# Cross-shaped window attention: the halves of a score tile lose their mutual waits on VectorE, and TensorE's steps are put in another order

## Chip, core and metric

The kernel runs on one core of one Trainium2 chip. The metric is the device time of one execution in microseconds (us); of several runs the median is given. TensorE (PE in the profile) does the matmuls, ScalarE (ACT) the exponentials, VectorE (DVE) and GpSimd (POOL) the elementwise work, and SyncE (SP) starts most of the DMAs.

## The reference

The input is one image `x` of 224 x 224 tokens with 96 channels. One matmul gives q, k and v. The first 48 channels are attended to within 28 horizontal stripes of 8 rows, the last 48 within 28 vertical stripes of 8 columns. A stripe has 1792 tokens, and each of its tokens attends to all 1792. Cut to what matters:

```
qkv = einsum('bhwc,cd->bhwd', x, wqkv);  q, k, v = thirds of qkv
scale = 48 ** -0.5
# horizontal: stripes of 8 x 224 tokens, channels 0..47
ah = softmax(einsum('bqc,bkc->bqk', qh, kh) * scale);  oh = einsum('bqk,bkc->bqc', ah, vh)
# vertical: stripes of 224 x 8 tokens, channels 48..95
av = softmax(einsum('bqc,bkc->bqk', qv, kv) * scale);  ov = einsum('bqk,bkc->bqc', av, vv)
out = einsum('bhwc,cd->bhwd', concat(oh, ov), wo)
```

The exponentials are the bulk of it: 56 stripes of 1792 x 1792 scores.

## The kernel before

**Passes and tiles.** Two stripes make a pass, and there are 28 passes: 14 horizontal, then 14 vertical. Within a pass the query columns are cut into four chunks (512, 512, 512, 256). A score tile is 128 keys of both stripes against one chunk, 128 partitions x 1024 columns: columns 0 to 511 belong to the one stripe, 512 to 1023 to the other. A pass has 49 tiles. Of these, 41 go to ScalarE, which takes `exp` of the whole tile in one instruction (L796). The other 8 go to VectorE and GpSimd, which work out an exponential by a polynomial: six of kind P and two of kind R, 224 tiles in all.

**The polynomial tiles.** VectorE takes each in halves of 512 columns, one half for each PSUM bank; `emit_p` records one such half. Pass p1 (L834) reads a bank and writes a half of a buffer `qb`. For kind R, pass p2 (L836) reads the same bank and that half of `qb` and writes a half of the tile `PT`. Then GpSimd works on all 1024 columns (`mids`: L846, L849 and L850 for kind P, L848 for kind R). Later TensorE computes the scores of the tile a second time, into two banks, and pass f (L839) joins them with `PT`. So VectorE has 448 instructions of p1, 112 of p2 and 448 of f.

**Waits.** Nothing is waited for by address. `Sched.commit` records each instruction with the keys that it reads and writes; `deps` turns them into waits on a counter of each engine. An instruction of VectorE that writes a key which VectorE wrote before waits for that earlier one too: only TensorE is let off waiting for itself. A `fresh` key forgets its past. Before the change, one buffer `qb` has one key, `("q", n)`, and one tile `PT` has one key, `("PT", slot)`, whichever half is touched.

**Order.** TensorE's steps stand in the strings of `ORDER`, one letter a step: `q` the scores of a ScalarE tile (L635), `1` and `2` the first and second scores of a polynomial tile (L648), `v` the product with V (L661), `k` a step that prepares the next pass (L437, L454, L483, L501), `f` a step of the output projection (L537, L573). The other engines' orders follow from it: as the letters are gone through, a planner with assumed durations (`D_H` for a half) and due times (`dve_step`, `pool_step`, `advance`) decides in which order VectorE and GpSimd take what has become ready. All engines then run their queues in order and wait on the counters.

**Buffers.** ScalarE's tiles use two sets of two PSUM banks. Four banks (`RING`) serve all the rest; `1` and `2` take two of them at once, and they come free as VectorE reads them out (L834, L836, L839, L813, L459, L470, L508, L443, L552, L585). There are 24 tiles `PT` and 5 buffers `qb`.

**DMAs.** SyncE's queue, in order, loads `x`, writes the transposed `x` to DRAM in the horizontal passes and reads it back in the vertical ones, and writes the output rows after L585; the last few output rows alternate between SyncE's and ScalarE's queue.

Of the kernel before, what the change touches and what calls it, by code (L numbers as in the profile page):

```python
# [30 lines left out]
D_MM, L_MM, L_PV, L_FILL = 0.216, 0.465, 0.44, 0.215  # L31
W_PE, W_FIN = 0.021, 0.08
SEMD, SEMP, SELF, SEMX = 0.15, 0.10, 0.19, 0.05
D_H, D_SQ, D_AF, D_ML = 0.6, 1.9, 1.03, 2.08


COLD = 8.0
# [3 lines left out]

KIND_OF = [0, 0, 0, 0, 0, 0, 0, 0, 0, 0, 0, 0, 0, 0, 0, 0, 0, 0, 0, 0, 0, 0, 0, 0, 0, 0, 0, 0]
ORDER = [
    "kqkqkkq11qkqkq1qvvvqkvqqkvq1vqkkqvkq1qkkqkq2qvkvq2vqv2qkvq1qvqvvvqvvq2qkvvqkvq1vvq2qvvq2kqvkv1qqvkkqvvkqvvkq2qvvkvq1qvkv",
    "fqv2qvvq1vqv1qvqvkqvvqvfqvvq1kqvq1fqvvvq1vqvvqvvq2qvkq2qkvq2qkvqv2qvvvqv1qvkqkvqvkq2kvq2qkvvqkq1vqkvkqffqvvvqkkqvvvfq1qvvvq2vk",
    "qvq2vvkqq1vvvvqkq1vqvqvkqkvq1qvv2qvfqvkvqvfqv1qvkqvvkq1qkvvvqkq2qvvq2qfkvqvqk1qvvfqkvqv2qfvqv2qvq1vqkvvfq2qvvkvq2qvvvvvkqq2vvfqk",
    "vvq1vvq1qvvkq1qvvvqvvqkvqkq1vqv1qvq2vvqv2qvqkq2vvvq1qvvvvqkqvvvqkkqfkqvvq2kq1qkvvqkqfvq2vvq1qvvkq2qvkvqkvkq2qvvvqffqvvkqvvvq1qv",
    "1qkqkvq2vqv1qvvfqvvqfqvvqkvq1fqvvq1vqv2q2qvvqv2qvv1qvqvvqvkq1qvv2qkqvvvfq2qvvvkqvqk2qvkvvq1qvvvkq2qkvvqkkvvqqkvkvv1qfqvvvkqv2qkvvq",
    "1qvffqvkqv1qvvqvvqvvq1vqkq1vqv2qkvqv2qkqvffqkvqvfqv2qvvq1vfqvqvvvqvvvq2qkvvq1qvvkkqfqv2qvkqfvq2vvq1qvkvqv2qkqkvqkvqvfq1vvqvkqvkkvv",
    "v2qvq1vvqffqkqvvvq1vqkvvqqkvkvq2q1qvvq2vvq2vqvkkvq1qvvkvq1qkvvvvqfkqvvqv2qvq1vvq2fqqkvvffqvvq1vq2qvkqvvq1qkkqkq2vvvq1qvvvkq2qkvvq1",  # L50
    "vqvkqvvqvvq1vvqffqvkqkkvq2qvvvq2vqvkkqkvvq1qkvvq2vvqvfq2vqvvfqvvq1qkvqvqvkvq1vq1qvkqv2qkvqv1qvkqvkq2qvkvq1qfvqvvvq2fqvvvqvkvq2qvv1",
    "qqvvvqv1qkqvvq1qvkq1vqvvqkqkfqvq2vqkvqkkvqv2qvvkqv2qvvq2vqkqvkq1vqkvqv2qvvvqv1qkqvkvq2fqvvqkvqvf1qvvqvkqv2qvvvq2qvvkfqvvfqv1",
    "qvqvkq2qvfqv1qvvqvvqvkqvfqv2qvkqvkq1qvvkvq1qvkvq2vqv1qvvqvvqkqfvkqvvq2vqkvq1vqv2qvkqfvqv1qvkqkvq2qvvfqvffqvvqkvqvkq2vqvkqvkf",
    "fqkvqvq1vvq1qvvkq2qvvkqvkq1qvvvqvvq1qvv2qvvq1qvkvq2qvvkq2qvkqfkvvq1qvvvqkqvvq1vvkqvq2vkqvq2vkqvvkq2qvvv1qkvqvvq2qkvvqv1qkvvvq1qv",
    "v2qfqvv1qvqvkqvqvk1qqkvvkq1qvv2qvvq1vvqvfqvkqvvqfkqvkvqkvq1kq2qvvv2qfqvkvqkqvvq2vqv2qkvqv1qvkqvkvq2qvvfqv2qvvvqk1qvvqkvvqfffqvvvqv",
    "1qvkqvkq2qkfqvvq2vqkvq1qvvqvvqv1qvvqkfq2qvvkqkqvkkqvvq1kq2qvkvfqvvq1qvvqvvvqkqk1qvvvq1qvvvq2kqvvq2vqvkq2vqvkqkvvq1fqvvvvq1qfvv",
    "q1qvvqvvq2vq2qvvq1qvvfqvvq2vqv2qvvq2fqvvkqvq1vfqvkqvkqv2qvvq1vkqvvvqkqv1qvvqvvkq2qkvvq2qfvvvq1qvvkqv1qvvfqkqvvvkq2qvvvkqvkfqvq2",
    "vvvq1qfvvvq1qvvqvvvq1qvqvkvq2qvfq2qvvkq2qvq1qkfqvv1qvqvvkqvvfqvq2vqkvvq2qvv1qvqkkfqfqvvvq2vqv1qkvqvqkvkqvkqvvq2vqvvkvq2fqvvvqv",
    "1qfvvqq1vvqfqvvqfvqv1qvvqvqvvq1vqkkvqkvq1q2qvq2q1qkvqvvvq2vqvvq1qvkfqvvqv2qkqvkvq2qkvvq1qvkvq2qvvkvq1qvvkvqvqvvvkq2fqvvvq",
    "v2qfqvvv1qvvq1qvfqvvvqqvvvqkqkk1qq2q1qvvvq2vvq1qvvqvvvq2qfvqq1vkqvvqf1qkqkkq2qvvvq2qvv1qfqvkqkvvvq2qvkvfqkqvvfqvqvv2vqfqkvvvv",  # L60
    "q1qvv2qfqvvvvq1qvvvvqfqqvvq1vvq2qkfqvvvq1qvvq1qvvvvqvq2vqvkq2qkvqkvq2vqv1qkvfqvq2vvqkkqv1qvq2vvq2qvvkqkkvvqq1vvkqvv1qvfqkvvvq2",
    "vqv1qvvqvqv1qvvqfvqvfqvvvq2qkkqvvqv2qvvvq1kqvq2vqv1qkvqvfqkqvq1vqvvvq1qkvqvv2qkqkqvv2qkvqkfqkvqvvq2qvv1qvvqvkqfvvqv2qvfqvv",
    "fqvqv2vqv1qvq1vvqvvqv2qvvqvqkkqkvfqkvqvfkqq1vvvvq1qvkvq2vqkvq2qvv1qvqvvqkvvq2qvq1vqfkqvvq2vvq2qvvq1vqkvvqkvfqvq2vvqvv1qkvqv2q",
    "vq1vq1qvvvqvqvvvq1fqvqfvqvvfqkvqqv2qvvq2qv2qvvkqfvq1vqvvqkvqkv2qkqvkq1vqvvqkqvvq1fqvq2vqkqv1qvvq2qvkqkvkqkvqv2qvvq1vvvq",
    "2qvv1qfvfqvvqfqvvvq1qvvvqvqvvvq1kqkq1qkqf2qvqvvqfkvvq2qvvvq2vq1qvvqvvqvq1kq1fqvqvvv2qvvq2kvqqkv2qkqkvvkq2qvvvvq2fqvvvkqfqvkvvqvvv",
    "q1fqvvq1vqvqv1qvvqvvvqvvq1qkkkqvvq2qvvkqv1vqv2qq1fqvqvvqkvq2vqv1qvq2qfvvqvqfvvq1vqvv2qfqvvvkqvkq2qkqkvvqvkkvq2qvvv2qfqvvvkvqfv",
    "qv1qvvvq1qfvqvfqvvqvvvkq1qvvqkvqvvqkv2qkvq1qvq2kq1qv2qq1qkvqvvvqkvq2qvvqkkvq1qfvvqv2qvvvq2qvkvvq1qvvvvqkvq2fqvvfqvvqkvvvq2qvv",
    "1qvvq1qfvvqvq1vqvvfqvq1qvqkvqvvkqkfqkvqv2qq1q1qvvqvvvq2qvq2kqv1qvvqkvvq1qvv2qvfqvkqvvq2vqvkq2qkvkqvkqkvqv2qvvq1vfqvvqfv",
    "vq2vqq1fqvvvq1vqvvqfqvvqvvvq2vqq1vqvkkqvkq2qkvq1qkfqvq2qfkqkvvqq2vvq1qkvqvvqvkvq2qvvvq1vvq1qvvkvq1qfvqvv2qvv1qvkqvqkvvv2qf",
    "vqvvq1qvvqvq2fqvqvv1qvq1qfvqvvvq2vqvv2qfqkvvqkvvqkqkvvq2kqvq1vkqvvqkqvvvq1vq1qvvqv2qvvq2vqkvqfvq2vqvkqvfqvvvvq2qvvkqvkq1vqvk",  # L70
    "1qfqvvvvq2vfqvvq1vqvvqqvvvq1vqv2q1qvvqv2qfvqvqfvfqvvq2qfqvvvq1fqvvqvqvvqv1qvvq2vvq1vvq2qvvv2qfvqfqfvfqvvfqvvfq2qvvvv2qfqvvvvvvfqvqffvvfvvvvfff",
]
MRG, LATE, BLATE = 0.01, 0.1, 0.05

# [98 lines left out]
def bass_standalone__window_attn_cswin__vision_kernel(  # L173
# [28 lines left out]
    with es:  # L202
        es.enter_context(nc.allow_low_precision(reason="sums for a mean key, which is taken off every key alike"))

        def sb(name, shape, dt):
            return es.enter_context(nc.sbuf_tensor(name, shape, dt))
# [19 lines left out]
        PT = [sb(f"PT{i}", [128, 1024], BF16) for i in range(NPT)]  # L226
        qb = [sb(f"qb{i}", [128, 1024], FP16) for i in range(NQB)]
# [13 lines left out]
        def bank(bi):  # L241
            return ps[:, bi * 512:(bi + 1) * 512]
# [3 lines left out]
        def low16(bi):  # L246
            return bank(bi).bitcast(I16).rearrange("p (n t) -> p n t", t=2)[:, :, 0]
# [14 lines left out]
        S = Sched()  # L262
# [516 lines left out]
        begun = set()  # L779

        def pt_keys(slot):
            return [("PT", slot)]
        pv_total = {c: len([1 for p in pv_chunks_of if p == c]) for c in range(NCH)}

        def emit_fill(f, bi):
# [8 lines left out]
        def emit_qk(tl, s, slot):  # L794
            S.commit("pe", 0.0, D_MM, L_MM, qk_fn(tl, s, 2 if 1 <= ia[0] <= NTWICE else 1), kt_keys(tl), set_keys(s), fresh=set_keys(s))
            S.commit("act", 0.0, D_ACT, None, lambda e, s=s, slot=slot: e.activation(  # L796
                PT[slot][:], ps[:, 512 * SETS[s]:512 * SETS[s] + 1024], ACTF.Exp, scale=LN2),
                set_keys(s), pt_keys(slot), fresh=pt_keys(slot))
# [29 lines left out]
        def emit_p(what, tl, h):  # L828
            bi, cols = tl["bp"][h], slice(512 * h, 512 * h + 512)
            q, y = qb[tl["qb"]][:, cols], PT[tl["slot"]][:, cols]  # L830
            bk, qk, ptk = [("bank", bi)], [("q", tl["qb"])], pt_keys(tl["slot"])
            if what == "p1":
                m, a = (HS * 2.0 ** -16, HS * RB) if tl["kind"] == "R" else (2.0 ** -16, 0.5 + PK)
                fn, reads, writes = lambda e: e.tensor_scalar(q, low16(bi), m, a, ALU.mult, ALU.add), bk, qk  # L834
            elif what == "p2":
                fn, reads, writes = lambda e: e.scalar_tensor_tensor(  # L836
                    y.bitcast(FP16), low16(bi), -RA * 2.0 ** 16, q, ALU.add, ALU.mult), bk + qk, ptk
            else:
                fn, reads, writes = lambda e: e.scalar_tensor_tensor(  # L839
                    y.bitcast(U16), bank(bi), 128.0, y.bitcast(FP16), ALU.mult, ALU.add), bk + ptk, ptk  # L840
# [45 lines left out]
        def dve_step():  # L886
# [304 lines left out]
```

## Time and profile before

| | |
|---|---|
| median of 3 runs | 1124.3 us (1120.11 to 1124.32) |
| the profiled execution | 1120.92 us; its span, first to last instruction, 1119.0 us |
| granted TensorE clock, mean | 0.995 |
| first and last ScalarE exponential | starts at 9.8 us, ends at 1111.0 us |
| L796, exponentials of 128x1024, ScalarE | 1148 instructions, 1076.5 us busy |
| L834 (p1), L839 (f), halves of 128x512, VectorE | 448 each, mean 686 and 687 ns |
| L836 (p2), VectorE | 112, mean 689 ns |
| HBM | 35 GB/s over the span |

An engine's busy time is the union of its instructions' spans. On VectorE and ScalarE an instruction may begin before the one ahead of it has ended, so an instruction's duration is more than the time that it takes from its engine; the time from one start to the next tells that. 1120.92 us is 1.9 us more than the span, and 3.4 us under the median.

### The profile page before, as it was taken

The page shows a single profiled execution, that of the slowest core. Times are in us where ns is not written, and L with a number is a line of the kernel's source. Part 1 is how long each engine was busy: PE and PEld are TensorE (multiplying, and loading weights), DVE is VectorE, ACT ScalarE, POOL GpSimd, SP SyncE. Part 2 cuts the span into 40 slices and gives each one's busy share as a digit, 9 for nine tenths or more (in the row PEclk, how much of TensorE's full clock was granted, in tenths as well). Part 3 has the DMA queues.
Part 4 walks back from the last instruction along what each step waited for, and adds up shares of the span by engine and source line. Part 5 has one row for each costly group of instructions (what it writes and reads, how often), then busy time and mean ns, then how long its engine had stood idle before and what let it go on. Part 6 is the DMA issues. An engine that isn't in the chain of part 4 may idle for free.

```text
span 1119.0 us, 36142 instructions
## 1 busy us (share of the span) xinstructions
PE 1071.9 (96%) x14928; PEld 428.7 (38%) x14928; DVE 1071.6 (96%) x2298; ACT 1081.1 (97%) x1159; POOL 955.8 (85%) x597
## 2 busy tenths in 40 slices
PE   9999999999999999999999989999999999999997
PEld 4344443443433443443333333333333343333332
DVE  8999999999999999999999999999999999999997
ACT  7999999999999999999999999999999999999996
POOL 7999789978888779979988998887989778897984
PEclk9999999999999999999999999999999998999999
DMA  5222123212302230321000112101111120121012
GB/s 93 38 50 52 20 33 51 43 17 45 52 11 42 52 51 2 52 42 36 2 26 15 35 20 53 38 19 45 46 40 23 41 52 11 46 47 41 17 25 38
DMA packets 183805, 40.97 MB, mean 37 GB/s; under 512 B 180408, under 2 KB 180952, under 8 KB 183640
## 3 DMA queue, kind: packets, MB, share of 16 engines
q1 hardware_dynamic: 182376, 38.14, 17.8%
q8 instruction: 117, 1.92, 0.7%
q10 hardware_dynamic: 1264, 0.52, 0.2%
q14 instruction: 48, 0.39, 0.1%
HBM read 19.36 MB, written 19.27 MB: 35 GB/s over the span
## 4 chain that ended last, share of the span: by engine, by line
DVE 46%; PE 40%; ACT 5%; issue 5%; POOL 3%; DMA 0%; DVEq 0%; ACTq 0%; POOLq 0%
PE ps L661 15%; DVE qb L834 14%; PE ps L635 13%; DVE PT L839 12%; PE ps L648 5%; ACT PT L796 5%; DVE out_all L585 5%; DVE PT L836 4%; PE ps L454 3%; DVE OT_sb L813 2%; DVE KT_sb L459 2%; DVE xT_sb L443 2%; PE ps L501 2%; PE ps L537 1%; DVE V_sb L508 1%
## 5 line engine op out<-in xcount | busy, mean ns | idle before, releaser
L796 ACT ACTIVATE PT<-ps 128x1024 bf16<-128x1024 f32 x1148 | 1076.5, 1041 | 25.7 <-PE ps L635 16.6
L635 PE MATMUL ps<-QT_sb,KT_sb 49*64 49x512 bf16 (+1 forms) x5420 | 477.9, 362 | 10.1 <-ACT PT L796 6.5
L661 PE MATMUL ps<-PT,V_sb 128*49 128x512 bf16 (+1 forms) x3136 | 455.2, 362 | 1.5 <-DVE PT L839 0.4
L846 POOL TENSOR_TENSOR PT<-qb 128x1024 f16<-128x1024 f16 x168 | 316.7, 1893 | 107.8 <-DVE qb L834 70.1
L850 POOL TENSOR_TENSOR PT<-PT,qb 128x1024 f16<-128x1024 f16 x168 | 355.5, 2124 | 9.1
L839 DVE SCALAR_TENSOR_TENSOR PT<-ps,PT 128x512 uint16<-128x512 f32 x448 | 305.7, 687 | 14.0 <-PE ps L648 4.9
L834 DVE TENSOR_SCALAR qb<-ps 128x512 f16<-128x512 int16 x448 | 305.6, 686 | 11.1 <-PE ps L648 4.9
L635 PEld LDWEIGHTS ps<-QT_sb,KT_sb 49*64 49x64 bf16 x5420 | 147.6, 104 | 256.8 <-ACT PT L796 199.9
L661 PEld LDWEIGHTS ps<-PT,V_sb 128*49 128x49 bf16 x3136 | 134.1, 103 | 197.3 <-issue 152.3
L648 PE MATMUL ps<-QT_sb,KT_sb 50*64 50x512 bf16 (+2 forms) x1792 | 181.6, 395 | 18.2 <-DVE qb L834 3.9
L849 POOL TENSOR_SCALAR PT<-PT 128x1024 f16<-128x1024 f16 x168 | 175.3, 1043 | 14.3
L848 POOL TENSOR_TENSOR PT<-PT 128x1024 f16<-128x1024 f16 x56 | 106.0, 1893 | 15.4 <-DVE PT L836 11.2
L585 DVE SCALAR_TENSOR_TENSOR out_all<-ps,rc,Ph_sb 128x96 bf16<-128x96 f32 x392 | 97.5, 306 | 0.6
L648 PEld LDWEIGHTS ps<-QT_sb,KT_sb 50*64 50x64 bf16 (+2 forms) x1792 | 51.0, 104 | 107.1 <-DVE PT L839 31.4
L836 DVE SCALAR_TENSOR_TENSOR PT<-ps,qb 128x512 f16<-128x512 int16 x112 | 77.1, 689 | 4.2
L813 DVE CAST OT_sb<-ps 113x512 bf16<-113x512 f32 x112 | 68.7, 613 | 0.2
L470 DVE CAST QT_sb<-ps 128x512 bf16<-128x512 f32 (+1 forms) x111 | 66.9, 611 | 2.1 <-PE ps L454 1.9
L459 DVE TENSOR_SCALAR_CACHE_REDUCE KT_sb<-ps 128x512 bf16<-128x512 f32 x108 | 64.0, 613 | 0.2
L552 DVE TENSOR_TENSOR Ph_sb<-ps,rc 128x480 bf16<-128x480 f32 (+1 forms) x84 | 52.0, 619 | 1.4
L508 DVE CAST V_sb<-ps 128x480 bf16<-128x480 f32 (+1 forms) x84 | 50.2, 615 | 1.7 <-PE ps L501 1.5
L454 PE MATMUL ps<-xT_sb,wq_sb 97*64 97x512 bf16 x224 | 41.2, 369 | 1.2 <-DVE wq_sb L487 0.6
L454 PE MATMUL ps<-xT_sb,w_sb 97*64 97x512 bf16 x224 | 40.1, 370 | 1.5 <-DVE out_all L585 0.5
(63 smaller groups left out, 395.0 us busy)
## 6 DMA issues: line engine op xcount, KB each, us to landing
xT_sb<-xt_dram SPq DMA_DIRECT2D x28, 336.0 KB, 3.9
out_dram<-out_all SPq DMA_DIRECT2D x385, 24.0 KB, 1.9
out_all<-in_x_dram SPq DMA_DIRECT2D x52, 168.0 KB, 2.7
xt_dram<-xT_sb SPq DMA_DIRECT2D x26, 336.0 KB, 6.0
xt_dram<-xT_sb SPq DMA_DIRECT2D x4, 168.0 KB, 4.5
Ph_sb<-in_x_dram SPq DMA_DIRECT2D x2, 168.0 KB, 3.8
Ph_sb<-in_x_dram ACTq DMA_DIRECT2D x2, 168.0 KB, 4.0
out_dram<-out_all ACTq DMA_DIRECT2D x7, 24.0 KB, 1.9
```

The lines of the kernel that those rows point to most:

```text
L454: ins = e.matmul(bk[64 * w:64 * w + 64, 0:qs], lhsT=lw, rhs=xT_sb[b][:, w, q0:q0 + qs], start=True, stop=True)
L585: return e.scalar_tensor_tensor(out_sb[b][:, w, kt, :], bk3[:, s, 0:C], rc[ri][:, s:s + 1], Ph_sb[:, kt, j, :], ALU.mult, ALU.add)
L635: ins = e.matmul(bank(SETS[s] + w)[64 * kh:64 * kh + 64, i * t["qs"]:(i + 1) * t["qs"]], lhsT=KT_sb[b][64 * w:64 * w + CA, kt * 128 + 64 * ...
L648: ins = e.matmul(bank(bp[w])[64 * kh:64 * kh + 64, 0:512], lhsT=KT_sb[b][64 * w:64 * w + nr, kt * 128 + 64 * kh:kt * 128 + 64 * kh + 64], ...
L661: ins = e.matmul(bank(pb)[64 * w:64 * w + CA, 0:t["qs"]], lhsT=V_sb[b][:, w, kt, :], rhs=PT[slot][:, ca:ca + t["qs"]], start=st and i == 0 ...
L796: S.commit("act", 0.0, D_ACT, None, lambda e, s=s, slot=slot: e.activation(PT[slot][:], ps[:, 512 * SETS[s]:512 * SETS[s] + 1024], ACTF.Ex ...
L834: fn, reads, writes = lambda e: e.tensor_scalar(q, low16(bi), m, a, ALU.mult, ALU.add), bk, qk
L836: fn, reads, writes = lambda e: e.scalar_tensor_tensor(y.bitcast(FP16), low16(bi), -RA * 2.0 ** 16, q, ALU.add, ALU.mult), bk + qk, ptk
L839: fn, reads, writes = lambda e: e.scalar_tensor_tensor(y.bitcast(U16), bank(bi), 128.0, y.bitcast(FP16), ALU.mult, ALU.add), bk + ptk, ptk
L846: sq = lambda e: e.tensor_tensor(y, q, q, ALU.mult)
L849: af = lambda e: e.tensor_scalar(y, y, PB, 128.0 * PA, ALU.add, ALU.mult)
L850: ml = lambda e: e.tensor_tensor(y, y, q, ALU.mult)
```

## The change

The key of a buffer `qb` and the key of a tile `PT` are split in two, one for each half. `emit_p` reads and writes the keys of its own half alone; GpSimd (`mids`), ScalarE and TensorE (`pt_keys`) name both. `fresh` now clears the key of each half with that half's first write. `D_H`, the planner's duration of a half, goes from 0.6 to 0.608. `ORDER` is replaced as a whole: it has the same 3531 steps (1148 `q`, 224 `1`, 224 `2`, 1372 `v`, 387 `k`, 176 `f`) in another order, and with it the orders of VectorE, GpSimd and SyncE move. The number of instructions stays the same on every engine, and one output row goes from ScalarE's DMA queue to SyncE's (7 and 385 become 6 and 386).

```
-D_H, D_SQ, D_AF, D_ML = 0.6, 1.9, 1.03, 2.08
+D_H, D_SQ, D_AF, D_ML = 0.608, 1.9, 1.03, 2.08
...
 ORDER = [
-    "kqkqkkq11qkqkq1qvvvqkvqqkvq1vqkkqvkq1qkkqkq2qvkvq2vqv2qkvq1qvqvvvqvvq2qkvvqkvq1vvq2qvvq2kqvkv1qqvkkqvvkqvvkq2qvvkvq1qvkv",
...
+    "kkqkkq1qkqkkq1qvqkvq1kvqqvvkvqkq1qkvq1qkqkv2qvqk2qkvqkqv2qvvkq1qvvvqkvqvq1vvq1qkvqv2qvvq2vqkv2qvqkkqvkkqvvvvq2qkvvvqv2qvv",
...
         def pt_keys(slot):
-            return [("PT", slot)]
+            return [("PT", slot, 0), ("PT", slot, 1)]
...
         def emit_p(what, tl, h):
...
-            bk, qk, ptk = [("bank", bi)], [("q", tl["qb"])], pt_keys(tl["slot"])
+            bk, qk, ptk = [("bank", bi)], [("q", tl["qb"], h)], [("PT", tl["slot"], h)]
...
-            S.commit("dve", 0.0, D_H, D_H + SEMD, fn, reads, writes, fresh=writes if h == 0 and what != "f" else [])
+            S.commit("dve", 0.0, D_H, D_H + SEMD, fn, reads, writes, fresh=writes if what != "f" else [])
...
         def mids(tl):
...
-            qk, yk = [("q", tl["qb"]), "pser"], pt_keys(tl["slot"])
+            qk, yk = [("q", tl["qb"], 0), ("q", tl["qb"], 1), "pser"], pt_keys(tl["slot"])
```

More of the change, by code (lines that the diff above doesn't have):

```diff
@@ L43 @@
 ORDER = [
-    "kqkqkkq11qkqkq1qvvvqkvqqkvq1vqkkqvkq1qkkqkq2qvkvq2vqv2qkvq1qvqvvvqvvq2qkvvqkvq1vvq2qvvq2kqvkv1qqvkkqvvkqvvkq2qvvkvq1qvkv",
-    "fqv2qvvq1vqv1qvqvkqvvqvfqvvq1kqvq1fqvvvq1vqvvqvvq2qvkq2qkvq2qkvqv2qvvvqv1qvkqkvqvkq2kvq2qkvvqkq1vqkvkqffqvvvqkkqvvvfq1qvvvq2vk",
-    "qvq2vvkqq1vvvvqkq1vqvqvkqkvq1qvv2qvfqvkvqvfqv1qvkqvvkq1qkvvvqkq2qvvq2qfkvqvqk1qvvfqkvqv2qfvqv2qvq1vqkvvfq2qvvkvq2qvvvvvkqq2vvfqk",
-    "vvq1vvq1qvvkq1qvvvqvvqkvqkq1vqv1qvq2vvqv2qvqkq2vvvq1qvvvvqkqvvvqkkqfkqvvq2kq1qkvvqkqfvq2vvq1qvvkq2qvkvqkvkq2qvvvqffqvvkqvvvq1qv",
@@ L48 @@
[L48 to L71, printed above, removed]
+    "kkqkkq1qkqkkq1qvqkvq1kvqqvvkvqkq1qkvq1qkqkv2qvqk2qkvqkqv2qvvkq1qvvvqvkqvq1vvq1qkvqv2qvvq2vqv2qkvqkkqvkkqvvvvq2qkvvvqv2qvv",
@@ new lines @@
+    "q1vvq1qkvqvkq1vqkqvvqvvfqvvq1qkq1q2kqvvvq1qvvvqvvq2vqvkqfvq2vqv1qvvqv2qkvvqvkq2kqvffqkvqkfqvvq2qvvq1kqvvvq2qvkvqkfqvvkvq1qk",
+    "vvfqkvq2qkqffqvq1qv1qvqvkqvvq2q1qvvvvq1qvkvvq2qvvkvq1qvkvqvvqvkqv2qvfqkvvvq2qvvvvq1qkvvq2qkvvvq2qvvvkq1qkvfqkvqkvqkvvq1qvkvvqvfq2",
+    "vqkvq1qkvq2qvvffqvqvv1qkqkfqvqvvqv2qvvvq1fqvvkqvq2vvq2qvvkqkvq1qvvkq1kqvqvkvqvfqkqkkqvq1vqv2qvkvqkfqvkvvq1qv2qvvq2vvq1qvvvvvfq",
+    "qkvv2qvvqf1qvvvq2vqv1qvqkqq1qkqvvvq2vqv1qvvq2qk2qvqkvvkqkvq1qkvvvvvfqfqvvvvqfvq1qkvq2vvq2qvkvvqffqvvvkq1qvkvvq2qvkqkvvvvq2qvkvvvkvqfq",
@@ new lines @@
+    "v1vqv2qkqvvvqf1qkfqvqvkq2qkvq1qvvvqvvqv2qvq1qv1qkvqkvkqvq1vkqvqv2qvvqv1qvkq2qkvvvq2qvvkqv1qkqvv2qkqkvvq1qfvvqkkqvvq1vvvq1q",
+    "vvvvq2qqkkvq1qfvvfqq2vvq1qvv1qvvqkvqvvvqv1qq2kvqvvkq2vvq2qvvvkq2qkvvfqvfqkvvqv1qkvq2qvkvfqvqv2qvkqkqkkvq2qvkvvfqfqvkvvvqf1qvvvq1qvvq",
+    "1vqvvvqvq2vvq1qvvvvqffqvvvq2vvq2qkqvv2qkqkvq1qvv1qvqkvqvvq1vqv2qvvvq1kqfqvvqkkvqvvkq2qvkvq2fqvvvqkkqkqvvq2vqkvvqkvvq2qvvvkkqvvq1vqvv",
+    "1qvqkvvq1qvvkqvqvkqkq1vfqvvq2fq2qvqvv1qvq1vqkvqvvvqv2qvvfqv1qvqkvqvvkq2qvkfqvv2qvvq1qkfqv2qvvkqkvq1qfvvqvvkq2qvvvfqkqkvkqkfqvv1v",
@@ new lines @@
+    "qq2vkqvkq1vqvvqvvqkqfvq1vqkvq1vqv1qvvqvvqkvq2qvvq2vvqkkqv2qvvq2qvv1qvvqv1qkvvq2qkvvqffqvvkqkqv2qvkvq2qvvkvqfqvvvkqvkkqvvfq2qvv",
+    "v1qvq1fqvkqvvq1fqvvvqvvqkqkq1vqvkq2fqvvvqkvq2vqv2qvvq1vfqkqvvkq2qkvvvq1qkvvqvfqvvvq1qvkvqv2qvvq2vvq1qkvqkkqvvqkq2vqvvkqkvvfq2qvvvv1",
+    "qvqkfqvvqfkq1qkfqqv1qvvqvvqv2qvq1qkq1vqv2qvvq1vqkvvqvqkvqv2qfvqvvkqvkq2fqvvvvq2qkvvvq1qvv1qvkqvkq2qkvqvvqkvkqffqvvvkq1qkvv",
+    "qkvkq2vqv2qvvq1vqvvq1vqkqvvvqv2qvvqk1qkqfvqv2qfvqkvvq2qkvvvq1qkvvq1vkqvqvkvq1qvvvqkvq2vvvq2qvvkfqvvq2vqv1qkqkvvqkqvkfqkvvq2vqvvfqv2",
@@ new lines @@
+    "qvvq1qv1qvq1qvvvqvvqv1qfvqvfqv1q1qvqvvkqvvqvq2qvv1qkqvv2qvq2qkvvqv1qvvqkvq2kvq2qvvkqkvqffqvvkvq2qvkvqkvvqk1qvvvqffqvkvvvqfq",
+    "2qv1qvq2vqvffqvvqv1qvvvqvvqv1qvq2vqv1qvq2qvvkq1qvvqvvkqfq1qvvfqq2vqkvqvv1qvvq2qvvkvq2qvvkq2kqvfqvkqvkq1vqkqkvkvq2qvvvkvqfqvv",
+    "2qvvq1qvv1qvvqvvqvvq1vqfvqvvvqkq2fqkvqvvvq2vqvkqkvq2kq1qkvq1qvvqvvqvvkq2qkvvqv1qkqvv2qvvq1vqv2qvvq1vqkfqvkvqvvqvv2qfqvvvfqvkvqv",
+    "2qvvq1fqvvqvvq1vqvvfqvvqkqvvvqv2qvq1vqkvq2vvq2qvv1qkqvv1qkvqkqq1vvqvq1vqfkqkvqv2qvvq2vqkvq2qfvqkvkqvvq1q2qvvvfqkqvvvkqvfq2vv",
@@ new lines @@
+    "qvvq1qvvvq2vqv1qvvqfvqvvqv1qvvqv2qvvkqfkqvkqvvq2vqvvkq1vqvq1vqfqvvqvvqv1qfqq2vqvv2qfqkqvkq2vvq2qvvqk1qkqvfqkvvqkkqvq1vk",
+    "vqfqvv1qvvvq2qvv1qvqvvvq1qvvvqv1q2qvvqkvkq1qvvqvvq2qvv2qvfqkvvqkvfqkvqvvq1qkvfqkqvvvq2qfvvq2qvvq1vvq2qkvkqkqkvvvvq1qvvv1qkvvq2qvv",
+    "vq2fvqvfqvvvvqvvv1qvfqqqq2qkq1qfvqvkvvq1qkvqv1qkvqvkqvq2vvq2qvv2qkvqkqvvq1vvq1qvkfqvvqv2qvkqkvq2fqvqvkvqv1qfqvvvq2vqkvvfqv",
+    "q1vqvvq2vq2qvv1qvqvvvq1qvvvqv1qq22qvqvv1qvvqvqkvq1vqfkqvvvq2vqvkqv1qvvkqvfqkvq2qkvvq2vfqvvvq1qvvkqkvvq2qvvvq2vkvqq1vvkqkvkvvqfqvvv1",
@@ new lines @@
+    "qvvqvvq2qvvvqv1qvq1vvq2q2qvvq1vqvqkvvqfkqfqvvqvkqkvvq2kq1fqvvqvvq1vqfvqv2qvqvvkq2qvfqvvqvkqk2qvvqvvqf2qvvvqvq1kqvkqkvfqkv",
+    "vqvv1qfqvvvvqfvq1vqvvvqq1qfq2qvqvkqkvq2qvkvq2qvv1qfqkvvq2qvvvq1vqvfqvvqvkqv1qvvq1qkkqfvq2qvvvqkq2qv1qkvqvvkqkfqvvvvq2qvvvvk",
+    "q2fqvq1qvvqvvq1vqvvqvvvqk2q1qvqvkvq1vqkq1qvvqvvvq2vqv2qfqvvkqvvq1qvfqvvvq2qvkqv2qvvq1vvq2qkvvqkqv2qkvqkvqkvqkfqkvvq2vq",
+    "v1qvq1vfqvvqfvvqfvq1qvvqvqvvvqv1q2qvvvq1qvv1qqvkvqvvqk2qvvq2vqkvqkvq1vvqv2qfqkvvq2qvvkqv2qvvq1fqvvvqkqkvqk1qvvvq2qvvkqvvkqkfqv",
@@ L72 @@
+    "v2qvvq1qfvqfvvqvqv1qvvqvvqv1q2q2qvvqv2qvq1vvkqkqkvq1qvvvvqfkqvvqv1qkq1fqvvvqvv2qvqkkvq2qfvqvv2qvvvq1qvkqvvvkq2qvvvkvq2qkvvfqvkvq",
+    "v2qvfqvvvvq1qvvvvq1fqvvvqq1qq1qq1qvvqvq2qvv2qvqkvkq1qvkqfkvqvvq2qfkqvvvq1qvkvvq2qvv2qkvkqfqkvvvqvvq2fqvvvvq2vqvvkq1qvvkfqvkq",
+    "v1qvvqv1qvvvqvvqv1qvfqq2vqvfq1qvvvqv1qfqqvvvq2qvvqv2qfvqqv1qvvvq2vfqvvq2qvvfqvvq2vvq1qvvq2vqvvffqvfqvvffqvfqvvvq2vqvffqvvqvvfqffvvvvfvff",
 ]
```

## The prediction

> **What bounds the kernel now.** I read the page's busy times first, then VectorE's instructions in order of time, then TensorE's waits at the score steps, then two passes side by side. The page:
>
> ```profile
> PE 1071.9 (96%) x14928; PEld 428.7 (38%) x14928; DVE 1071.6 (96%) x2298; ACT 1081.1 (97%) x1159; POOL 955.8 (85%) x597
> DVE 46%; PE 40%; ACT 5%; issue 5%; POOL 3%; DMA 0%; DVEq 0%; ACTq 0%; POOLq 0%
> L796 ACT ACTIVATE PT<-ps 128x1024 bf16<-128x1024 f32 x1148 | 1076.5, 1041 | 25.7 <-PE ps L635 16.6
> L839 DVE SCALAR_TENSOR_TENSOR PT<-ps,PT 128x512 uint16<-128x512 f32 x448 | 305.7, 687 | 14.0 <-PE ps L648 4.9
> ```
>
> Three engines look full, and the chain of waits runs through VectorE most. Busy time doesn't tell them apart, since it counts waits inside a pair of instructions as well. VectorE in order of time does (start, length, instruction, count):
>
> ```profile
> 705.21 0.68 DVE L470 CAST QT_sb<-ps 128x512 bf16<-128x512 f32 x1
> 705.81 0.65 DVE L508 CAST V_sb<-ps 128x480 bf16<-128x480 f32 x1
> 706.41 1.42 DVE L834 TENSOR_SCALAR qb<-ps 128x512 f16<-128x512 int16 x2
> 707.74 2.73 DVE L839 SCALAR_TENSOR_TENSOR PT<-ps,PT 128x512 uint16<-128x512 f32 x4
> 710.39 1.11 DVE L508 CAST V_sb<-ps 128x480 bf16<-128x480 f32 x2
> ```
>
> L470 lasts 0.68 us, yet its successor starts after 0.60: instructions overlap. The pair L834 takes 1.33 us to the next start, the four L839 take 2.65, so not 2 or 4 times 0.61. By the starts, a half followed by an instruction that does not wait for VectorE gives its place up after 0.608 us (medians 607 to 609 ns); a half directly followed by its own second half, which waits for it, after 0.715 to 0.717 (L834 to L834, 159 times; L839 to L839, 165) or 0.725 (L836 behind L834 or L836, 84). So the wait costs 0.11 us each time.
>
> VectorE's load is the sum of its start-to-start times without waits: 1008 halves x 0.608 = 613; 248 copies of 512 columns x 0.60 = 149; 83 of 256 x 0.333 = 28; V 45; L552 45; 392 L585 x 0.225 = 88; reciprocals, transposes' copies and the rest 47. That is 1015 us. To this come 408 x 0.11 = 45 of waits between halves and about 11 of other waits of VectorE for itself (L544 to L552, L580 to L585): 1071 us, 97% of the 1101.2 us between the first and the last exponential. ScalarE's exponentials follow each other at 0.903 or 0.920 us when nothing holds them, 0.912 in the mean: 1148 x 0.912 = 1047 us, 95%. So VectorE is the fuller by 24 us. TensorE feels it at the score steps:
>
> ```profile
> L648 PE MATMUL ps<-QT_sb,KT_sb x1792: 377/400/631, 11.5 to 1106.1; 50*64 50x512 bf16 x96, 52*64 52x512 bf16 x78, 53*64 53x512 bf16 x26
> its engine sat idle before it (us, times) until:
>   DVE PT L839: 33.7, 103
>   DVE qb L834: 29.7, 83
> ```
>
> Matmuls and their weight loads are counted here together. By TensorE's starts, 448 score steps begin 44 us late in all against their usual distance from the step before (about 0.10 each), of some 137 us late over all steps. TensorE without lateness would need about 970 us. It is not the bound; its in-order queue passes VectorE's lateness on to the next `q`.
>
> Two vertical passes, cut at the starts of their first exponentials, show both regimes (busy times are PE, PEld, DVE, ACT, POOL):
>
> ```profile
> 678.20:718.00 39.80, 38.56 (x508) 14.87 (x504) 39.17 (x90) 38.49 (x43) 32.45 (x19) 1.00 0.15 36
> 718.00:755.70 37.70, 36.91 (x500) 14.02 (x496) 36.21 (x87) 37.68 (x43) 34.19 (x22) 1.00 0.17 38
> ```
>
> In the first VectorE is full and ScalarE has holes; in the second ScalarE is full and the pass is 2.1 us shorter. 41 exponentials need 37.4 us, so 37.7 is nearly the least that a pass can be.
>
> **The change, part by part.**
>
> *Separate keys.* In the two built programs I counted VectorE instructions that wait for the instruction directly ahead of them: before, 159 of L834, 84 of L836 and 165 of L839; after, none on those lines. What is left is 112 waits of L836 for its own half of p1, at least one instruction back, mostly with another half (0.608 us) between; the written half is then 1.2 us old, more than the 0.717 that a waiting pair needs. These cost nothing; where the cover is a reciprocal of 0.1 us, as before some halves now, it would be 0.02 us. So VectorE's load falls by 45, to 1026 us, or 1.6 us a pass. It also frees the second bank of a pair 0.11 us earlier.
>
> [...]
>
> *ScalarE.* The same 1148 exponentials: 1047 us. It becomes the fullest engine, so at most 24 of the 45 us count at once.
>
> *`ORDER`.* Mode switches between the 64-row steps (`q`, `1`, `2`, `f`) and the others go from 1819 to 1797. A step of 4 matmuls behind one of its kind takes about 0.22 us and behind a change 0.31 to 0.34, so 22 x 0.1 = 2 us of TensorE, off the bound: I take 0. The distances between `q` steps are as before (3 steps 476 times for 479, 6 or more 14 for 12). From a score step back to the step that fed the VectorE instruction it waits for, the mean is 5.54 steps for 5.48. GpSimd keeps its 956 us, 85%, and `1` stands a median 42 steps ahead of its `2` for 40.5: room enough. What an order alone is worth no row shows. I bound it by passes: mean 39.3 us, best 37.7, worst 41.5, without the lead and tail. A different arrangement of each pass could lie anywhere there; averaged over 28 I take 0, with 10 us either way for the range.
>
> *DMAs.* The reads of transposed `x` land in 3.9 us; the first `k` that needs them stands 23 steps or more behind the start of the pass before (22 or more now), at 0.31 us a step 7 us. Before, no TensorE wait on a DMA shows outside the lead. Output rows move on SyncE's queue with their `f`; that queue is in order, but its loads are followed by 3 us of room: 0, and 0 to 3 us if one load per pass came late in a few passes. The one row moved from ScalarE's to SyncE's queue costs 0 to 2 us at the end (a row lands in 1.9). Lead (9.8 us) and tail (8.0) keep their length.
>
> *The sum*, two ways. (1) Now 1101 - 1071 = 30 us are lost beyond the fullest engine. If as much is lost beyond ScalarE: 1047 + 30 + 17.8 = 1095 us of span. (2) The 26 inner passes, sorted by VectorE's load: the eight least loaded (mean 36.8 us) last 38.3, the nine most loaded (39.5) last 40.0; a line through all falls by 0.64 us per us of load. 1.6 us less gives 28 x 1.6 x 0.64 = 29 us: 1090. I take 1094, nearer to (1), since two engines will stand within 2% of each other. With 1.9 us outside the span that is 1096 for an execution like the profiled one; the median of the runs lies 3.4 above that one, so 1096 to 1099, and I say **1098 us**.
>
> **The rivals.** *The gain does not arrive.* Either the second half starts no earlier, because VectorE's pipeline empties behind every half, waited for or not, and its 1071 us stay; or ScalarE's holes come from TensorE's long steps (20 small matmuls for V take 0.4 us, 16 transposes 0.49) and not from VectorE. Then a span of 1119 plus or minus 5, a time of 1119 to 1129. For it: in the passes that start at 328 and 367 us ScalarE loses 1.1 to 1.3 us although VectorE has 1.5 to 2.5 us free. Against: the two distances in the starts, and the two passes above. 0.08, of it 0.02 for the pipeline. [...]
>
> *Slower: scores put too early.* A `1` or `2` that stands one step (1101 / 3560 = 0.31 us) before its two banks are free stops TensorE, and the `q` behind it, for that long. Against a gain of 25 us, 80 of 448 score steps so placed cancel it. At 125, 39 us go: 1121 - 25 + 39 = 1135 us. For it: the steps back are no more than before, while each step is meant to be shorter; and an order made for exact pitches leaves less room. Against: VectorE's pairs are also shorter, and the pitch assumed, 0.608, is the one in the trace, whereas before the planner's VectorE (`dve_step`) left out the 0.11. 0.13.
>
> **How the numbers follow.** Forecast 0.79, no gain 0.08, slower 0.13. Half a percent, about what a measurement of this kernel can tell from no change, is 1119 to 1130; so faster 0.79, same 0.08, slower 0.13. Low end: every pass at the mean of the best four now, 38.0 us: 28 x 38.0 + 17.8 = 1082, and 1084 with what lies around. High end: the gain of 24 reduced by order (10) and a late load (3) gives 1110; to leave out no more than 0.2 it goes on to 1119, where the case without gain begins.
>
> **What would show it.** Right: mean of L834 and L839 still near 690 ns but pairs 1.30 us long instead of 1.42; VectorE's busy time near 1026 to 1035 us of some 1094; its share of the chain below 46%, ScalarE's and TensorE's above; ScalarE's idle time under 25.7 us; the waits of L648 for VectorE down. Wrong: pairs still 1.42 long (no gain), or TensorE's idle time before L648 grown while VectorE sits idle waiting for L648 (the order).

## The result, and the profile after

The changed kernel takes 1113.25 us (median of 4 runs, 1112.17 to 1114.25); beside it, the kernel before took 1124.31 us (4 runs, 1120.11 to 1126.16). The ratio is 0.9907, with a 95% interval from 0.9877 to 0.9936. The gain, 0.9%, is clear of the noise, and under half of the 2.3% that was forecast. The profiled execution took 1113.59 us, with a span of 1111.8 us.

The page, by the same lines as before: busy times, the chain, the exponentials and pass f, and the granted clock in 40 slices.

```profile
PE 1071.8 (96%) x14928; PEld 430.5 (39%) x14928; DVE 1047.4 (94%) x2298; ACT 1072.5 (96%) x1159; POOL 955.0 (86%) x597
PEclk9999999999999999999999989998999999999598
PE 62%; ACT 18%; DVE 12%; issue 4%; POOL 1%; DMA 1%; ACTq 0%; DVEq 0%; SPq 0%; POOLq 0%
L796 ACT ACTIVATE PT<-ps 128x1024 bf16<-128x1024 f32 x1148 | 1068.1, 1062 | 26.5 <-PE ps L635 22.1
L839 DVE SCALAR_TENSOR_TENSOR PT<-ps,PT 128x512 uint16<-128x512 f32 x448 | 290.6, 683 | 23.0 <-PE ps L648 18.4
```

VectorE's share of the chain fell from 46% to 12%, TensorE's rose from 40% to 62%. ScalarE's holes did not shrink (26.5 us for 25.7), and VectorE now waits for the score steps L648, 18.4 us ahead of L839 where it was 4.9. And the clock row has three dips ahead of its last slice. VectorE in order of time:

```profile
689.51 1.28 DVE L834 TENSOR_SCALAR qb<-ps 128x512 f16<-128x512 int16 x2
690.70 1.28 DVE L836 SCALAR_TENSOR_TENSOR PT<-ps,qb 128x512 f16<-128x512 int16 x2
700.39 2.49 DVE L839 SCALAR_TENSOR_TENSOR PT<-ps,PT 128x512 uint16<-128x512 f32 x4
702.79 0.68 DVE L813 CAST OT_sb<-ps 113x512 bf16<-113x512 f32 x1
```

Pairs are 1.28 us long for 1.42, and four L839 take 2.40 us to the next start for 2.65: 0.60 each. So the waits between halves are gone, and a pair gives its place up sooner, as was said. Five passes side by side, cut at their first exponentials (stretch, length, then PE, PEld, DVE, ACT, POOL, the granted clock, DMA share, GB/s):

```profile
625.90:672.00 46.10, 42.38 (x500) 14.30 (x498) 37.93 (x91) 38.91 (x42) 35.88 (x22) 0.85 0.15 33
672.00:709.70 37.70, 36.28 (x500) 14.23 (x496) 36.85 (x90) 37.66 (x42) 28.67 (x18) 1.00 0.19 42
748.20:789.40 41.20, 38.94 (x509) 14.77 (x504) 38.52 (x98) 38.42 (x43) 34.67 (x22) 0.92 0.11 21
979.90:1018.40 38.50, 37.57 (x512) 15.17 (x508) 38.26 (x93) 38.24 (x42) 36.52 (x22) 1.00 0.18 38
1018.40:1064.90 46.50, 44.91 (x510) 15.98 (x508) 39.07 (x96) 39.20 (x42) 30.67 (x18) 0.74 0.15 33
```

Three passes, and only these, ran at a lowered clock. In the trace the granted clock stands at one half from 634.4 for 13.65 us, from 757.3 for 6.83 us and from 1027.0 for 23.89 us. These passes last 46.1, 41.2 and 46.5 us; the other 25 last 38.4 in the mean. 133.8 - 3 x 38.4 = 18.6 us are lost in them; the span without that is 1093 us, and the forecast had 1094. Before, one stretch of 6.83 us (at 930.1) lay between the lead and the tail. TensorE ahead of the first and the second of the three (in brackets, idle time and what ended it):

```profile
632.14 0.41 PE L635 MATMUL ps<-QT_sb,KT_sb 49*64 49x512 bf16 x4
635.38 0.64 PE L454 MATMUL ps<-xT_sb,w_sb 97*64 97x512 bf16 x2 [2.83 <-DMA xT_sb<-xt_dram]
635.95 0.64 PE L635 MATMUL ps<-QT_sb,KT_sb 49*64 49x512 bf16 x4
```

```profile
754.73 0.41 PE L635 MATMUL ps<-QT_sb,KT_sb 49*64 49x512 bf16 x4 [0.51 <-ACT PT L796]
755.64 0.41 PE L635 MATMUL ps<-QT_sb,KT_sb 49*64 49x512 bf16 x4 [0.51 <-ACT PT L796]
756.56 0.41 PE L635 MATMUL ps<-QT_sb,KT_sb 49*64 49x512 bf16 x4 [0.29 <-ACT PT L796]
757.48 0.64 PE L635 MATMUL ps<-QT_sb,KT_sb 49*64 49x512 bf16 x4 [0.17 <-ACT PT L796]
```

The first is a read of transposed `x` that lands late: on SyncE's queue it stands behind 13 output rows, and TensorE stops for 2.83 us. The second is no stop at all: for 3 us TensorE has little but one `q` for every exponential, and waits for ScalarE between them. From 757.3 on the same matmuls last 0.64 us for 0.41. The third is like the second: TensorE waits in turn for ScalarE and VectorE, and no pause is over 0.4 us. In neither of the two is a product with V issued for 3.4 us. All three times the clock falls 8.5 to 9.1 us after the first exponential of a vertical pass.

### The profile page after: what moved, and what is told of

It reads as the page before. It is cut to its first block, busy times and chain, and to the rows that moved or that the text cites. A ratio compares the mean times of both kernels' runs of the same rounds, so it can differ in the third digit from the quotient of the medians.

```text
span 1111.8 us, 36150 instructions
## 1 busy us (share of the span) xinstructions
PE 1071.8 (96%) x14928; PEld 430.5 (39%) x14928; DVE 1047.4 (94%) x2298; ACT 1072.5 (96%) x1159; POOL 955.0 (86%) x597
## 4 chain that ended last, share of the span: by engine, by line
PE 62%; ACT 18%; DVE 12%; issue 4%; POOL 1%; DMA 1%; ACTq 0%; DVEq 0%; SPq 0%; POOLq 0%
PE ps L661 23%; PE ps L635 22%; ACT PT L796 18%; PE ps L648 7%; PE ps L454 4%; DVE qb L834 3%; DVE PT L839 3%; PE ps L501 2%; DVE out_all L585 2%; PE ps L437 1%; PE ps L537 1%; PE ps L573 1%; DVE OT_sb L813 1%; DVE PT L836 1%; PE ps L483 1%
## 5 line engine op out<-in xcount | busy, mean ns | idle before, releaser
L796 ACT ACTIVATE PT<-ps 128x1024 bf16<-128x1024 f32 x1148 | 1068.1, 1062 | 26.5 <-PE ps L635 22.1
L635 PE MATMUL ps<-QT_sb,KT_sb 49*64 49x512 bf16 (+1 forms) x5420 | 484.0, 367 | 19.0 <-ACT PT L796 14.0
L839 DVE SCALAR_TENSOR_TENSOR PT<-ps,PT 128x512 uint16<-128x512 f32 x448 | 290.6, 683 | 23.0 <-PE ps L648 18.4
L834 DVE TENSOR_SCALAR qb<-ps 128x512 f16<-128x512 int16 x448 | 291.2, 682 | 12.2 <-PE ps L648 9.6
L648 PE MATMUL ps<-QT_sb,KT_sb 50*64 50x512 bf16 (+2 forms) x1792 | 183.0, 397 | 7.0 <-DVE PT L839 1.8
L648 PEld LDWEIGHTS ps<-QT_sb,KT_sb 50*64 50x64 bf16 (+2 forms) x1792 | 51.9, 105 | 76.2 <-DVE PT L839 22.4
L836 DVE SCALAR_TENSOR_TENSOR PT<-ps,qb 128x512 f16<-128x512 int16 x112 | 73.0, 680 | 0.0
L454 PE MATMUL ps<-xT_sb,w_sb 97*64 97x512 bf16 x224 | 43.2, 383 | 2.9 <-DMA xT_sb<-xt_dram 2.8
```

The costliest lines, as they stand in the source:

```text
L454: ins = e.matmul(bk[64 * w:64 * w + 64, 0:qs], lhsT=lw, rhs=xT_sb[b][:, w, q0:q0 + qs], start=True, stop=True)
L635: ins = e.matmul(bank(SETS[s] + w)[64 * kh:64 * kh + 64, i * t["qs"]:(i + 1) * t["qs"]], lhsT=KT_sb[b][64 * w:64 * w + CA, kt * 128 + 64 * ...
L648: ins = e.matmul(bank(bp[w])[64 * kh:64 * kh + 64, 0:512], lhsT=KT_sb[b][64 * w:64 * w + nr, kt * 128 + 64 * kh:kt * 128 + 64 * kh + 64], ...
L839: fn, reads, writes = lambda e: e.scalar_tensor_tensor(y.bitcast(U16), bank(bi), 128.0, y.bitcast(FP16), ALU.mult, ALU.add), bk + ptk, ptk
```

## The experiments

**Theories.** C: the price of the waits was right; most of the gain was given back to stretches of half TensorE clock, which the new order brings about by leaving TensorE with little to do for 3 us and more. O: the new order is the worse one by itself, and the clock only goes with it. N: the waits of VectorE were not what held the others up. All times are medians unless said otherwise; clocks are means over a run. Each ratio is taken against the kernel before as it ran beside that group of experiments: 1119.2 us beside 1, 2 and `both`, 1121.6 beside the four kernels of 4, 1122.4 beside `both_few`, `keys_few` and the late read, against 1124.3 beside the changed kernel. So times of different groups compare to a few us only.

**1. The keys alone, and the order alone.** The two halves of the change were run each without the other. `keys_only` is the kernel before with the four edits of keys; no instruction moves on any engine.

```
-            return [("PT", slot)]
+            return [("PT", slot, 0), ("PT", slot, 1)]
...
-            bk, qk, ptk = [("bank", bi)], [("q", tl["qb"])], pt_keys(tl["slot"])
+            bk, qk, ptk = [("bank", bi)], [("q", tl["qb"], h)], [("PT", tl["slot"], h)]
```

> The separate keys in the order of before (D_H 0.6, old ORDER): every engine's instructions stand as before, only VectorE's waits between halves are gone. Theory C (the waits cost what they were priced at, and the changed kernel lost most of its gain again to stretches of half TensorE clock, which cost it some 19 us): VectorE's load falls by 45 us, pairs of L834 and L839 1.30 us long, time 1092 to 1105 us if no more than one stretch of half clock falls in, and some 3 to 9 us more for each further stretch. Theory O (the new order is what lost the gain, the clock only goes with it): 1092 to 1100 us whatever the clock does. Theory N (the waits were worth little, VectorE was not what held the others up): 1112 to 1120 us.

Measured: 1103.62 us (4 runs, 1097.38 to 1105.85), ratio 0.9826 (0.9766 to 0.9887). `order_only` has the opposite edits, made in the changed kernel:

> The new ORDER and D_H with the old keys: VectorE waits between halves again. Theory C: VectorE carries 1071 us again and is the fullest engine, 1116 to 1130 us, within 1% of before; fewer or shorter stretches of half clock than in the changed kernel, since TensorE waits less for ScalarE. Theory O: the new order is worse than the old by itself, 1130 to 1140 us. Theory N: no more than 4 us from the changed kernel, 1112 to 1117 us.

Measured: 1138.83 us (1132.71 to 1141.49), ratio 1.0141 (1.0080 to 1.0203). N is out: the keys alone gain more than the whole change, and the order alone loses. C missed the second by 9 us, since its condition failed too: four stretches of half clock instead of fewer, 61 us together. Two passes of that run:

```profile
995.20:1043.80 48.60, 47.29 (x512) 16.23 (x510) 40.78 (x93) 39.70 (x43) 36.09 (x21) 0.75 0.14 30
1043.80:1088.50 44.70, 42.32 (x510) 15.40 (x508) 39.92 (x96) 39.48 (x43) 30.59 (x18) 0.81 0.15 35
```

So the long falls, of 13.65 us and more, came with the new order under either keys. The old order is not free of them: `keys_only` had three short ones, 17 us together, in its profiled execution. By the numbers C has the first run and O the second; both stand.

**2. The late read put earlier.** In `queue_prep` the reads for a vertical pass are queued one pass sooner.

```
             if P >= NPH:
-                plan_x(P)
+                [plan_x(z) for z in ((P, P + 1) if P == NPH else (P + 1,)) if z < NP]
```

> The changed kernel with each read of transposed x for the vertical passes put on SyncE's queue one pass earlier, so that it no longer stands behind output rows right before it is needed; orders of the other engines unchanged. Theory C: the 2.8 us wait of TensorE for the read at 632 us goes, and with it the 13.7 us of half clock behind it; the pass at 626 us lasts 38 to 39 us for 46.1; the other two stretches stay; 1104 to 1108 us. Theory O: only the 3 us of the wait itself come back, 1109 to 1111 us.

Measured: 1104.1 us (1096.62 to 1108.23), ratio 0.9852 (0.9786 to 0.9917), 9 us less than the changed kernel had in its own group. Within the traces the pass at 626 us went from 46.1 to 38.2 us, 7.9 us less, of which the wait itself was 2.8:

```profile
625.50:663.70 38.20, 37.17 (x500) 13.97 (x498) 37.48 (x91) 38.04 (x43) 35.73 (x22) 1.00 0.18 39
739.70:780.80 41.10, 39.03 (x512) 14.90 (x508) 38.51 (x98) 38.56 (x43) 34.77 (x22) 0.92 0.13 26
```

The single runs put time and clock in one line: 1096.62 us at a clock of 0.994, 1102.69 at 0.987, 1105.51 at 0.983, 1108.23 at 0.980, about 0.8 us for each thousandth. `keys_only` does the same: 1097.38 at 0.998, 1102.07 at 0.991, 1105.16 and 1105.85 at 0.987. The third stretch (1027 us before) did not come in the profiled execution, which is this kernel's fastest.

**3. TensorE kept at work.** Some score steps issue their four matmuls twice, with the same values, where TensorE waits for ScalarE anyway. Both kernels do so already for their first 11 tiles; the tiles below come on top. Each costs 0.22 us of TensorE.

```
-            S.commit("pe", 0.0, D_MM, L_MM, qk_fn(tl, s, 2 if 1 <= ia[0] <= NTWICE else 1), kt_keys(tl), set_keys(s), fresh=set_keys(s))
+            S.commit("pe", 0.0, D_MM, L_MM, qk_fn(tl, s, 2 if ia[0] in TWICE else 1), kt_keys(tl), set_keys(s), fresh=set_keys(s))
```

With early reads and 15 tiles (`both`):

> As the kernel with early reads, and the score matmuls of 15 ScalarE tiles (numbers 784 to 790 and 1071 to 1078) are issued twice with the same values, which keeps TensorE at work in the two stretches before the clock fell at 757 and 1027 us; it waits there for ScalarE anyway. Theory C: no half clock between the lead and the tail, passes at 748 and 1018 us 38 to 39 us for 41.2 and 46.5, 1093 to 1099 us. Theory O: the added work costs its 15 x 0.22 = 3 us or nothing, and the time stays within 3 us of the kernel with early reads alone.

Measured: 1098.95 us (1098.66 to 1099.95), ratio 0.9795 (0.9744 to 0.9847). With added work the median is 5 us lower, and the runs lie within 1.3 us instead of 12. The gain is that the longer runs stay away: the fastest run of `early_loads`, 1096.62 us at a clock of 0.994, lies 2 us or more below every run of `both`, whose clocks are 0.993 and 0.994. The stretches at 757 and 1027 us are gone; a new one of 6.83 us came at 866 us, so the low end of the expectation was not reached. Ten tiles more, ahead of that place (`both_few`):

> The new order with early reads and 25 tiles issued twice: numbers 784 to 790, 909 to 918 and 1071 to 1078; the ten in the middle are added ahead of the half clock that was left at 866 us with 15 tiles. Theory C: 1094 to 1098 us, within 3 us of the old order with 21 tiles, so the new order is no better than the old at full clock. Theory O: 1099 us or more.

Measured: 1097.88 us (5 runs, 1097.33 to 1099.25), ratio 0.9783 (0.9763 to 0.9803). This is the lowest median of all versions. Its clock row is whole up to the tail, and ScalarE's holes are down to 11.3 us:

```profile
PEclk9999999999999999999999999999999999999998
L796 ACT ACTIVATE PT<-ps 128x1024 bf16<-128x1024 f32 x1148 | 1066.4, 1062 | 11.3 <-PE ps L635 6.9
```

**4. Keys and order at full clock.** Four kernels, old and new keys by old and new order, all kept warm: 75 tiles more are doubled in the old order (`before_warm`, `keys_warm`), 101 in the new (`order_warm`, `after_warm`, both with early reads).

> The kernel before, with the score matmuls of 75 ScalarE tiles more issued twice (same values), in places where TensorE waits for ScalarE and its work in 3.4 us is small. Theory C (time is set by the granted clock on top of the load of the fullest engine): clock 0.998 or more, 1115 to 1119 us, since before lost only 1 to 3 us to the clock. Theory O (the clock goes with the stalls and costs nothing of its own): no change from before, or some us slower for the 75 x 0.22 = 16 us of added TensorE work.

> Separate keys in the old order, with the same 75 tiles issued twice. Theory C: clock 0.998 or more in every run, 1094 to 1099 us, a narrow spread; 4 to 10 us less than the separate keys alone (1103.6). Theory O: 1103 to 1108 us.

> The new order with the old keys, reads of x one pass earlier, and 101 tiles issued twice. Theory C: the order by itself is worth nothing at full clock, 1113 to 1120 us at a clock of 0.995 or more, against 1138.8 us without these two additions. Theory O: the order is worse than the old by itself, 1128 to 1138 us.

> The changed kernel, reads of x one pass earlier, and 101 tiles issued twice. Theory C: clock 0.998 or more, 1093 to 1098 us, as the old order with separate keys and warm stretches, within 4 us of it. Theory O: 1099 us or more, since more work is added than in the kernel with 15 tiles issued twice.

| | old order | new order |
|---|---|---|
| one key for a buffer | 1121.9 us, clock 0.998 to 0.999 | 1124.2 us, clock 0.993 to 0.998 |
| a key for each half | 1102.45 us, clock 0.998 to 0.999 | 1103.52 us, clock 0.998 to 0.999 |

The keys are worth 19.4 us in one order and 20.7 in the other. The kernels of the new order are 1 to 2 us slower; that holds the order, the early reads and 26 more doubled steps together, and `order_warm` still has one stretch of half clock in its trace. That is C in the main, and O falls: nearly without half clock the new order is as good as the old within 2 us, against 20 us in experiment 1. All four lie above the ranges of C by 3 to 6 us, where O had placed the first and the last. So many doubled steps do cost: beside `before_warm`, the kernel before had two runs at 0.997 and one at 0.999 of the clock, and they took 1117.95 to 1119.92 us, 2 to 4 us less. With the separate keys it may be 5 us (`keys_only` had 1097.38 us in its one run at 0.998, in another group). A smaller dose in the old order (`keys_few`, 21 tiles):

> Separate keys in the old order, with 21 tiles issued twice for 75: numbers 680 to 685, 872 to 880 and 962 to 967, ahead of the three stretches of half clock that separate keys alone showed at 649, 830 and 916 us. Theory C: those stretches go, clock 0.996 or more, and less is paid for added work: 1095 to 1100 us. Theory O: 1102 to 1105 us.

Measured: 1101.18 us (6 runs), ratio 0.9826 (0.9795 to 0.9858), so above C's range by 1 us, and inconclusive against `both_few`, which also has early reads. Five runs lie between 1100.15 and 1103.07; the sixth, 1112.23, shows the clock from another side. Full clock came only at 34.9 us, where the other runs' traces have it at 4 to 10 us, though TensorE worked without a pause over 0.05 us from 11.8 us on, and its first pass lasted 49.3 us instead of the 39.6 to 39.9 of `keys_only` and `keys_warm`. Eight matmuls of 512 columns took 1.06 us there:

```profile
13.23 1.07 PE L635 MATMUL ps<-QT_sb,KT_sb 49*64 49x512 bf16 x8
14.08 1.06 PE L648 MATMUL ps<-QT_sb,KT_sb 50*64 50x512 bf16 x8
14.94 1.06 PE L635 MATMUL ps<-QT_sb,KT_sb 49*64 49x512 bf16 x8
```

**5. A standstill on purpose.** In `keys_warm`, the read for one vertical pass is given one more key, so that it starts only when TensorE has finished the step ahead of its first `k`.

```
+            if c == "k" and P == 20 and "late" not in S.wr:
+                S.note(("pe", S.cnt["pe"]), [], ["late"])
+                plan_x(P)
```

> The separate keys in the old order with 75 tiles issued twice (1102.5 us at a clock of 0.998 to 0.999, no half clock but at the end), and one thing more: the read of transposed x for one vertical pass starts only when TensorE has finished the step ahead of the first k that needs it, near 774 us, so TensorE stands still for the 4 us that the read takes to land. Theory C: the standstill itself costs 3 to 4 us, and behind it the clock falls to half for 7 to 14 us, which costs 3 to 8 us more; 1108 to 1115 us, clock 0.990 to 0.996. Theory O: no stretch of half clock, or one that costs nothing; 1105.5 to 1107 us.

Measured: 1110.71, 1112.16 and 1113.66 us, at clocks of 0.995, 0.992 and 0.993: 8 to 11 us above `keys_warm`, as C had it. A fourth execution, the profiled one, had 0.75 of the clock until 1079 us and 0.85 after that, with 13.65 us at one half behind the late read, and took 1209.74 us. The kernel once more, for a trace at full clock:

> The kernel with the one late read once more, for its trace: the profiled execution of the first time ran at three quarters of the TensorE clock from the lead on. Theory C: TensorE waits 4 to 5 us for the read near 774 us, the clock falls to half at the next boundary of a 3.41 us grid and stays so for 7 to 14 us, and the pass lasts 45 to 48 us for 38 to 39. Theory O: full clock behind the wait, and a pass of 42 to 43 us.

Measured: 1113.9 us, one run (the kernel before took 1134.61 us in its one run beside it, so only the trace is used here). The wait lay near 754 us, 20 us earlier than I had placed it. In order, TensorE at the wait; the pass with it; the same pass of `keys_warm`:

```profile
758.41 1.06 PE L454 MATMUL ps<-xT_sb,w_sb 97*64 97x512 bf16 x4 [4.53 <-DMA xT_sb<-xt_dram]
```

```profile
745.80:794.10 48.30, 43.07 (x496) 14.98 (x494) 38.52 (x89) 38.84 (x43) 31.55 (x19) 0.86 0.16 37
```

```profile
744.40:782.70 38.30, 37.96 (x496) 14.11 (x494) 37.63 (x88) 38.06 (x42) 31.44 (x19) 1.00 0.21 48
```

The clock fell at 757.1 us, within the standstill, for 13.65 us. The pass is 10.0 us longer: 4.5 of standstill, and 5.5 more, which I put down to the half clock; no run has a standstill of this length at full clock to compare. This is the shape of the stretch at 634 us of the changed kernel.

## Why the prediction was wrong in size

**The waits.** Right in price. In the old order the keys alone gave 1100.3 us of span in an execution with three stretches of half clock (17 us long), and at nearly full clock they were worth 19.4 and 20.7 us, where the sum had 24. The rival by which the pipeline would empty anyway is out: no run shows it, and halves follow each other at 0.608 us now (211 pairs of L839, median), where a waiting pair took 0.715 to 0.717.

One sign missed. VectorE's busy time was to be near 1026 to 1035 us, and it is 1045.7 in `keys_only` and 1047.4 in the changed kernel, 26 and 24 us less than before and not 45. Busy time does not measure those 45 us: in a waiting pair some 0.03 us counted as idle already (a length of 0.686 us, the next start after 0.714), and an instruction with a pause behind it counts with its whole 0.68 us instead of 0.60. Pauses of more than 0.04 us went from 120 to 209 in `keys_only`.

**ScalarE as the next bound.** Right where the clock was full: in the changed kernel 25 passes of 38.4 us against a least of 37.4, so the loss beyond the fullest engine is 1.0 us a pass, 28 in all. The first way of the sum had 30. The second way, the line through the passes, had 1090 of span, and no kernel got there: the fastest span is 1094.7.

**`ORDER`.** "A different arrangement of each pass could lie anywhere there; averaged over 28 I take 0, with 10 us either way" is the step that failed. At nearly full clock it holds (1 to 2 us). As the kernel was built, the order cost 18.6 us instead of 0, in three stretches of half clock of 44 us together, and the 10 us either way did not hold it. (The medians of the changed kernel and of `keys_only` differ by 9.6 us only, since the old order with separate keys had falls of its own.) The order also decides how evenly TensorE's work lies in time, and that I had not weighed: the page of before had a dip in its clock row, and the pass at 913 us stood at 41.1 us with a clock of 0.92, among the longest; the prediction does not mention it.

```profile
PEclk9999999999999999999999999999999998999999
913.00:954.10 41.10, 39.41 (x500) 14.68 (x498) 38.27 (x89) 38.65 (x42) 33.93 (x20) 0.92 0.16 35
```

Equal totals of steps, equal gaps between `q` and equal loops back to VectorE did not show it; the share of time in which matmuls stream does. I take the stretches of 3.41 us on whose edges the clock changes, and count 0.215 us from the start of a matmul of 512 columns (the shortest distance of one such step to the next in the trace), in proportion for fewer columns, and overlaps once. That share has a median of 0.73 in the changed kernel and 0.71 before. In the stretch ahead of each fall it was 0.32, 0.37 and 0.36 in the changed kernel, and 0.44 ahead of the one before. In the thirteen traces other than the one at 0.75 of the clock, up to the last exponential, all ten stretches under 0.45 were followed by a fall, 6 of 28 between 0.45 and 0.53, and none of some 4000 above that. So the share tells which stretches are in danger, but the edge is not sharp by this rough measure.

**DMAs.** "0 to 3 us if one load per pass came late in a few passes": it came late once, by 2.8 us, and cost some 8 with what it set off. (In `order_only` the same read came 2.3 us late, with the same 13.65 us of half clock.) The count of steps between the start of a pass and its first `k` was no margin, because the read's place on SyncE's queue was behind rows that leave late; I had the queue's order and did not follow that one read in it.

**The rivals.** Scores put too early did not decide: L648's idle entry for L839 fell from 33.7 to 24.2 us. What I had for "wrong" did show, VectorE waiting for L648 (18.4 us ahead of L839). Only 6 of the 18 lie in the three passes with half clock, and nearly without half clock it is 12.6 us in `both_few` and 14.7 in `after_warm`: a VectorE that is no longer the fullest engine waits anyway, so the sign could not tell the two cases apart. A small slip besides: the 3560 steps behind the 0.31 us a step are 3531, which changes nothing.

The lengths of half clock, 13.65, 6.83 and 23.89 us, are 4, 2 and 7 times 3.41. In each trace the changes between half and full clock lie on one grid of 3.413 us, and the grid lies otherwise against the first instruction from trace to trace (0.2 to 3.0 us past a multiple: 1.7 before, 3.0 in the changed kernel). No standstill was needed: ahead of the fall at 757.3 us TensorE ran a `q` every 0.91 us. The execution of 1209.74 us had two other values, 0.75 and 0.85 of the clock.

What stays open: why half clock lasted 23.89 us at 1027 us and 6.83 at 757 with much the same matmuls, and why runs of one kernel differ in the number of falls. That the grid lies otherwise against the kernel in each run might explain the second; no run here tests it.

## What to carry to other kernels

A wait of VectorE for its own last result cost 0.11 us on 0.61 each time here, and finer keys take it away without moving an instruction. When that makes another engine the bound, look at what the relieved ones do in the meantime: a TensorE that waited for 2.83 us, and one that waited for 4.53 us, ran at half clock for 13.65 us here. Follow each DMA to its place in its queue before calling it hidden, and read the clock row of each pass before comparing two orders.

## What the runs showed of the hardware

- TensorE's clock fell to one half without a standstill: ahead of the falls at 757 and 1027 us of the changed kernel no pause was longer than 0.51 us. In thirteen traces every stretch of 3.41 us in which matmuls streamed for under 0.45 of the time brought a fall, some up to 0.52 did, and none above 0.53; the clock stayed at one half for 3.4 to 23.9 us. One standstill of 4.5 us brought 13.65 us of half clock.
- Issuing matmuls twice to fill the light stretches lowered the median: from 1104.1 us to 1098.95 with 15 doubled steps and to 1097.88 with 25 (in another group). With 75 in the old order it stayed within 1.2 us (1121.9 for 1121.6, 1102.45 for 1103.62).
- At the start of one run the clock stayed at one half until 34.9 us, through 23 us of dense matmuls, and its first pass was some 9 us longer.
